# Block-causal attention with a bilinear feed-forward behind it: the softmax of a pair of heads written in eight short pieces, weight conversions written step by step, and constant products in the first five slots

## The chip, the cores and the metric

The kernel runs on one core of one Trainium2 chip. The metric is device time in microseconds (us) of one execution, the median of several runs. Lower is better.

## The reference

Sixty-four heads (8 batches of 8) attend over 576 positions of width 64, with a mask that lets a block of 64 queries see its own block and those before it. The heads of a position are put side by side, and a bilinear feed-forward of width 1536 follows.

```python
scores = scale * np.matmul(q, k.transpose(0, 1, 3, 2))
scores = np.where(block_i >= block_j, scores, -1000000000.0)   # blocks of 64
scores = scores - np.max(scores, axis=-1, keepdims=True)
attn = np.exp(scores)
attn = attn / (np.sum(attn, axis=-1, keepdims=True) + 1e-09)
attn_out = np.matmul(attn, v).astype(np.float32)
x = attn_out.transpose(0, 2, 1, 3).reshape(4608, 512)
a = x @ w_a            # 512 x 1536
b = x @ w_b            # 512 x 1536
return (a * b @ w_out).astype(np.float32)
```

## The kernel before

The heads go through in 32 pairs, two heads of 64 features on the 128 partitions. A loop over 34 **slots** (`for s in range(NP + LAG)`, L571) does three things in each slot `s`: the output products of pair `s-2` (`values`, L459), the transposes of pair `s-1` (`turn`, L437) and the scores and softmax of pair `s` (`softmax`, L366). Each of the three is a Python generator, and a table `SLOT` (L567) says in which order their next pieces are written; the third number of an entry is its weight in the slot's progress `now`, which runs from `2s` to `2s+2`.

Between the pieces stand products of the feed-forward's **first pass** (`first_pass`, L493): the first 4 of 12 blocks of 128 hidden features, for 16 half batches of 288 positions. For each block f, `ab_unit` (L234) makes a sum of 12 products for `a` and one of 12 for `b` in two PSUM banks of `ps_mm` (2 buffers, tag `mm`): ScalarE copies the first to SBUF (`a`, L247), VectorE multiplies the second with it (`hf`, L249), ScalarE rounds that (`hh`, L112), GpSimd takes the rest (`hl`, L115). After the first block of a half batch stand the output products of the half batch before (`o_unit`, L254), four sums of 12 products that ScalarE copies out (`ob`, L502). As there are two buffers, a new sum waits until the sum but one before has been read. `want(now)` (L555) sets how many products have been written at a given `now`: none before 10.2 (`MOE_FROM`, in slot 5), and 72 in each slot from slot 9 on. Slots come in two kinds by turns: one holds the second, third and fourth block of a half batch (six sums called `ps`), the other holds a first block and the output products (two `ps`, four `pso`).

In a slot, `softmax` writes first the scores of query tile 3 (`LAST`), of the side tile (`NT`, 64 queries at each end) and of tile 1, in four banks of `ps_sc` (L399 to L403). VectorE takes the row maxima (`top`, L388, tile `nm`; `nb` for tiles that share rows, L411), ScalarE the exponentials with their row sums (`exps`, L391): tile 3 of both heads (out `e`, bias `nb`, 128x512), the side tile of both (out `e_s`), then tile 1 (`e`, bias `nm`, 128x320) after a masking memset (L395). The second piece writes the scores of tiles 2 and 0 in the same four banks, their maxima and exponentials (128x448, 128x192), the reciprocals of the sums (`rc`, L430) and GpSimd's scaling of all exponentials by them (L434). `turn` is in seven pieces: up to four transposes with the identity (`tp`, L453, two buffers) and ScalarE's copy of them (`ah`, L456). `values` makes `av` (L471) from `ah` and `v`.

Pairs 0 to 5 use plain fp32 products for the scores (`NATIVE`), later pairs split q and k into rounded and rest parts (`split_qk`, L342: L348, L349 for q, L112, L115 for k).

The weights of the first pass are **converted** on the way in (`convert`, L129: five VectorE operations of 128x512 on a block and one ScalarE operation, then a rounding copy on ScalarE and a subtraction on VectorE, L110). They are 12 conversions of 5 steps; `CONV_PER_SLOT`, `CONV0` and the loop at L595 set how many steps have been written at a given `now`.

TensorE's instructions stand in program order (`PE_ORDER`, L542). The other engines' queues are ordered by a scheduler, which may put an instruction of later code ahead of one of earlier code; each engine then runs its queue in order. Before the loop stand 9 products of zeros into a `ps_mm` bank (`WARM`, L309).

After slot 33 come the rest of the first pass and the second pass (L769 on), which the change doesn't touch.

Of the kernel before, what the change touches and what calls it, by code (L numbers as in the profile page):

```python
# [9 lines left out]
F32 = mybir.dt.float32  # L10
# [7 lines left out]
P = 128  # L18
BLK = 64
NEG = -1.0e30  # L20
EPS = 1e-9
CONV_POOL = 1
CONV_POOL2 = 0
CONV_PER_SLOT = 1.0
CONV0 = 1
HL_DVE = False
MOE_FROM = 10.2
# [4 lines left out]
XQ = lambda nc: nc.scalar  # L32
PE_ORDER = ["PE"]
WARM = 9
KEEP = {}
NATIVE = 6

XFB = 2
# [16 lines left out]
def attention_then_bilinear_ffn(  # L55
# [10 lines left out]
    nc = tc.nc  # L66
# [202 lines left out]
    ps_t = psum(right, "ps_t", 1)  # L269
# [10 lines left out]
    nk = [min(P * t + 3 * BLK, S - BLK) for t in range(NT)]  # L280
# [4 lines left out]
    W = S - BLK  # L285
# [18 lines left out]
    if WARM:  # L304
        z = const.tile([P, W], F32R, name="z")
        nc.vector.memset(f32(z), 0.0)
        ps = ps_mm.tile([P, 512], F32, tag="mm", name="warm")
# [58 lines left out]
    def softmax(p):  # L366
# [3 lines left out]
        eb = [e_bufs[(2 * p + h) % NE] for h in range(2)]  # L370
        sm = s_bufs[p % 2]

        nm, rc = (apool.tile([P, 2, NT + 1], F32, tag=x, name=f"{x}{n}") for x in ("nm", "rc"))
        nb = apool.tile([P, 2, 2], F32, tag="nb", name=f"nb{n}")

        def banks(t):
            return [ps_sc.tile([P, 512], F32, tag="sc", name=f"s{t}{n}_{h}") for h in range(2)]

        def scores(t, outs):
            for j, (qq, kk) in enumerate(qk):  # L380
                for h, r in enumerate(rows):
                    keys = ends(kk[r]) if t == NT else kk[r, :nk[t]]
                    mark = nc.tensor.matmul(  # L383
                        outs[h], qq[r, q0[t]:q0[t] + P], keys, start=j == 0, stop=j == len(qk) - 1)
            return mark

        def top(t, h, view):
            nc.vector.tensor_reduce(nm[:, h, t:t + 1], view, axis=AX.X, op=ALU.max, negate=True)  # L388

        def exps(t, h, out, view, bias):  # L390
            nc.scalar.activation(out, view, AF.Exp, bias=bias, accum_out=sm[:, h, t, :1])  # L391

        def masked(t, ps):
            for h in range(2):
                nc.vector.memset(ps[h][:BLK, nk[t] - BLK:nk[t]], NEG)  # L395
                top(t, h, ps[h][:, :nk[t]])
                exps(t, h, eb[h][0][t][:, :nk[t]], ps[h][:, :nk[t]], nm[:, h, t:t + 1])

        ps = {t: banks(t) for t in (LAST, 1)}  # L399
        side = [x[:, nk[1]:nk[1] + P] for x in ps[1]]  # L400
# [2 lines left out]
        mark = scores(1, [x[:, :nk[1]] for x in ps[1]])  # L403
# [9 lines left out]
            nb[BLK:], two[BLK:, :, None, :].to_broadcast([P - BLK, 2, 2, 2]), axis=AX.X, op=ALU.min)  # L413
        for h in range(2):
            exps(LAST, h, eb[h][0][LAST], ps[LAST][h], nb[:, h, :1])
        for h in range(2):
            exps(NT, h, eb[h][1], side[h], nb[:, h, 1:])
        masked(1, ps[1])
        yield mark
        ps = {t: banks(t) for t in (2, 0)}  # L420
        for t in (2, 0):
            mark = scores(t, [x[:, :nk[t]] for x in ps[t]])
        for t in (2, 0):
            masked(t, ps[t])
# [120 lines left out]
    NP = NH // 2  # L545
# [9 lines left out]
    def want(now):  # L555

        n = (now - H - LAG) * per_slot - behind
        if now < 2 * H + LAG:
# [3 lines left out]
    keep = conv2 = None  # L562


    S_, T_, V_ = softmax, turn, values

    SLOT = [(V_, -2, 0), (S_, 0, 12), (T_, -1, 7), (T_, -1, 7), (T_, -1, 8), (S_, 0, 12), (T_, -1, 6),  # L567
            (T_, -1, 6), (T_, -1, 6), (T_, -1, 8)]
    fill = sum(m for _, _, m in SLOT)
    gens = {}  # L570
    for s in range(NP + LAG):  # L571
        if s == NP - 1:
            raw = fetch(wab[F1, :, 0], f"w{F1}_0")
        due = 0
        for k, (what, i, m) in enumerate(SLOT):
            i += s
            if 0 <= i < NP:
                mark = next(gens.get((what, i)) or gens.setdefault((what, i), what(i)))
                for _ in range(KEEP.get((s, k), 0)):
                    keep = keep or ps_t.tile([P, W], F32, tag="tp", name="keep", bufs=2)  # L580
                    nc.tensor.matmul(keep, z[:, :P], z, start=True, stop=True)
                marks.append(mark)
            if k == 0 and s < NP:
                load_v(s)
            if k == 5 and s + 1 < NP:
                split_qk(s + 1)
            if k == 5 and s + 2 < NP:
# [12 lines left out]
            while moe and n_moe < want(now):  # L600
                next(moe)
                n_moe += 1
# [137 lines left out]
    n_conv = n_conv2 - 1  # L740
# [8 lines left out]
    k = 0  # L749
# [16 lines left out]
    k = 0  # L766


    for ps_ in range(2):  # L769
        fs = list(range(F1 + ps_ * F2, F1 + (ps_ + 1) * F2))  # L770
        for tt in range(NT2):
# [23 lines left out]
            nm = f"z{ps_}_{tt}"  # L795
# [74 lines left out]
```

## Time and profile before

| | |
|---|---|
| median of 3 runs | 1299.45 us (1296.85 to 1302.84) |
| the profiled execution, its own time | 1300.42 us |
| its span, first to last instruction | 1298.6 us |
| TensorE (PE) busy | 1208.5 us, 93% |
| VectorE (DVE) busy | 790.7 us, 61% |
| ScalarE (ACT) busy | 620.6 us, 48% |
| GpSimd (POOL) busy | 351.9 us, 27% |
| DMA queues, mean | 104 GB/s |
| slots 0 to 33, until the last `av` ends | to 683.7 us |
| of it before the first pass's products are dense | to 128.6 us |

A row of a timeline has the start (us from the span's start), the duration, engine, line, operation, output<-inputs with the buffer numbers left out, and in brackets how long the engine had been idle before it and what released it. PEld is TensorE's weight load. A row of the waits has the waiting instruction, what it waited for, the total, how often, and the longest. A row of the windows view has a stretch, its length, the busy time of each engine with its number of instructions, the clock granted to TensorE as a share of full speed (PEclk), and the DMA load.

### The profile page before, as it was taken

What the parts mean: (1) busy time and instruction counts of PE and PEld (TensorE: products, weight loads), DVE (VectorE), ACT (ScalarE), POOL (GpSimd) and SP (SyncE); (2) the same over time, 40 slices, a digit from 0 to 9 for tenths busy, and PEclk for the clock granted to TensorE, in tenths of its full rate; (3) what the DMA queues carried; (4) which work ended last, traced back from release to release, by engine and by line L of the source; (5) the groups of instructions that cost most, each with busy time, mean ns of one, the idle gap of its engine ahead of it and who ended that gap; (6) DMA issues with size and microseconds to landing.
All of it is one profiled execution on the core that took longest, in us unless ns stands there. A gap on an engine that the chain in (4) does not pass through costs nothing.

```text
span 1298.6 us, 22050 instructions
## 1 busy us (share of the span) xinstructions
PE 1208.5 (93%) x8045; PEld 1098.4 (85%) x8045; DVE 790.7 (61%) x1932; ACT 620.6 (48%) x1550; POOL 351.9 (27%) x540
## 2 busy tenths in 40 slices
PE   5778998999999898999999989999999999999998
PEld 2446877778787787787889989999999999999998
DVE  6884444434344434444347999797788677677664
ACT  3656666565665656565554544453343322222210
POOL 1464454454535353444430001210220100000000
PEclk6677999999999999999999989999999999999999
DMA  5431222222222132212114426643668751353231
GB/s 188 135 127 49 77 87 68 86 59 77 68 86 80 57 95 68 86 59 77 39 54 138 138 80 173 157 119 98 159 162 275 213 147 51 96 147 89 58 97 61
DMA packets 68652, 135.65 MB, mean 104 GB/s; under 512 B 7616, under 2 KB 42432, under 8 KB 68544
## 3 DMA queue, kind: packets, MB, share of 16 engines
q1 hardware_dynamic: 57024, 115.37, 28.8%
q0 software_dynamic: 6912, 9.44, 4.7%
q10 hardware_dynamic: 4608, 9.44, 1.9%
q8 instruction: 63, 1.03, 0.4%
q14 instruction: 45, 0.37, 0.1%
HBM read 87.03 MB, written 47.19 MB: 103 GB/s over the span
## 4 chain that ended last, share of the span: by engine, by line
PE 74%; DVE 11%; ACT 11%; issue 3%; DMA 1%; SPq 0%; ACTq 0%; DVEq 0%
PE pso_z L722 14%; PE ps L223 9%; PE psw_z L676 7%; PE psx_z L676 7%; PE av L471 7%; PE pso L223 7%; PE psv_z L676 7%; PE s L383 6%; ACT e L391 6%; PE tp L453 5%; DVE nm L388 4%; PE psy_z L676 3%; ACT ah L456 2%; ACT e_s L391 1%; ACT a L247 1%
## 5 line engine op out<-in xcount | busy, mean ns | idle before, releaser
L223 PE MATMUL ps<-xh,wab 128*128 128x288 f32 x1024 | 230.4, 304 | 18.0 <-ACT a L247 18.0
L722 PE MATMUL pso_z<-h_z,wo 128*128 128x384 f32 x1152 | 204.3, 335 | 2.1 <-DVE u_z L703 2.1
L722 PEld LDWEIGHTS pso_z<-h_z,wo 128*128 128x128 f32 x1152 | 200.5, 188 | 2.5 <-issue 2.3
L223 PEld LDWEIGHTS ps<-xh,wab 128*128 128x128 f32 x1024 | 168.5, 188 | 28.4 <-ACT a L247 22.9
L434 POOL TENSOR_SCALAR e<-e,rc 128x512 f32<-128x512 f32 (+3 forms) x256 | 149.2, 602 | 129.5 <-DVE rc L430 127.8
L223 PE MATMUL ps<-xl,wab 128*128 128x288 f32 x512 | 158.5, 310 | 0.0
L456 ACT COPY ah<-tp 128x512 f32<-128x512 f32 x224 | 134.3, 604 | 40.0 <-PE tp L453 40.0
L388 DVE TENSOR_REDUCE nm<-s 128x1 f32<-128x512 f32 (+4 forms) x320 | 146.8, 484 | 10.3 <-PE s L383 6.3
L453 PE MATMUL tp<-ident,e 128*128 128x128 f32 x832 | 134.2, 285 | 9.9 <-ACT ah L456 6.9
L383 PE MATMUL s<-k,q 64*128 64x512 f32 (+3 forms) x900 | 113.1, 369 | 26.2 <-ACT e L391 25.8
L112 ACT CAST h_z<-u_z 128x384 fp32r<-128x384 f32 x96 | 49.3, 513 | 175.0 <-DVE u_z L701 159.6
L223 PE MATMUL pso<-hh,wo 128*128 128x288 f32 x480 | 106.1, 302 | 20.9 <-ACT ob L502 13.0
L383 PEld LDWEIGHTS s<-k,q 64*128 64x128 f32 x900 | 78.7, 193 | 52.4 <-ACT e L391 37.2
L453 PEld LDWEIGHTS tp<-ident,e 128*128 128x128 f32 x832 | 105.3, 146 | 18.7 <-issue 8.9
L785 POOL DMA_DIRECT2D part<-pt x48 | 42.6, 1056 | 288.6 <-ACT pt L784 288.4
L391 ACT ACTIVATE e<-s,nm 128x448 f32<-128x448 f32 (+2 forms) x192 | 102.5, 540 | 38.2 <-DVE nm L388 37.9
L676 PE MATMUL psx_z<-xh,wab 128*128 128x384 f32 x384 | 117.3, 341 | 3.5 <-DVE u_z L694 1.8
L676 PE MATMUL psw_z<-xh,wab 128*128 128x384 f32 x384 | 116.8, 339 | 0.0
L676 PE MATMUL psv_z<-xh,wab 128*128 128x384 f32 x384 | 116.1, 338 | 0.0
L480 DVE COPY xf<-av 128x512 f32<-128x512 f32 x32 | 22.1, 691 | 138.7 <-PE av L471 138.1
L471 PE MATMUL av<-ah,v 128*64 128x64 f32 (+4 forms) x768 | 99.4, 410 | 3.0 <-ACT ah L456 3.0
L223 PEld LDWEIGHTS pso<-hh,wo 128*128 128x128 f32 x480 | 78.5, 188 | 26.5 <-ACT ob L502 15.6
(112 smaller groups left out, 2284.3 us busy)
## 6 DMA issues: line engine op xcount, KB each, us to landing
xr<-xd SPq DMA_DIRECT2D x48, 384.0 KB, 4.4
raww<-wab SPq DMA_DIRECT2D x24, 512.0 KB, 3.8
v<-vm SPq DMA_DIRECT2D x64, 160.0 KB, 3.9
xd<-xf ACTq DMA_DIRECT2D x32, 288.0 KB, 3.8
part<-ob SPq DMA_DIRECT2D x64, 144.0 KB, 3.1
part<-pt POOLq DMA_DIRECT2D x48, 192.0 KB, 6.9
pt<-part SPq DMA_DIRECT2D x48, 192.0 KB, 3.4
outT<-pt SPq DMA_DIRECT2D x48, 192.0 KB, 3.5
```

What stands on the lines that cost most here:

```text
L112: nc.scalar.copy(hi, src)
L223: mm = nc.tensor.matmul(ps, w_, d_, start=(i == 0), stop=(i == n - 1))
L383: mark = nc.tensor.matmul(outs[h], qq[r, q0[t]:q0[t] + P], keys, start=j == 0, stop=j == len(qk) - 1)
L388: nc.vector.tensor_reduce(nm[:, h, t:t + 1], view, axis=AX.X, op=ALU.max, negate=True)
L391: nc.scalar.activation(out, view, AF.Exp, bias=bias, accum_out=sm[:, h, t, :1])
L434: nc.gpsimd.tensor_scalar(ev, ev, rc[:, h, t:t + 1], 1.0, op0=ALU.mult, op1=ALU.mult)
L453: mark = nc.tensor.transpose(tp[:, c], src, ident)
L456: nc.scalar.copy(ah[(slice(None), *at)], got)
L471: mark = nc.tensor.matmul(out[r], v[:, i, c], a[:, i, src, cols], start=start, stop=stop, skip_group_check=True)
L676: nc.tensor.matmul(ps, wt[:, i, iw], j[:, ix], start=start and kp == 0 and i == 0 and j is xh, stop=kp == KP - 1 and i == 1, skip_group_ch ...
L722: nc.tensor.matmul(ps, wt[:, a, osl], b, start=i == 0, stop=i == 3 * len(fs) - 1)
L785: nc.gpsimd.dma_start(part[o * P:(o + 1) * P, ts], t, accum_op=ALU.add)
```

## The change

`softmax` yields seven more times than at its scores' ends alone, so that it comes in eight pieces: tile 3 of the one head and all the scores and maxima before it; tile 3 of the other head; the side tiles and tile 1 of the first head; tile 1 of the second; the scores of tiles 2 and 0 with tile 2 of the first head; tile 2 of the second; tile 0 of the first; tile 0 of the second with the reciprocals and the scaling. The new `SLOT` has 16 entries (1 of `values`, 8 of `softmax`, 7 of `turn`), and products of the first pass stand behind each but the first; their number for a slot is the same. `split_qk` and `load_qk` come after the sixth piece instead of after the second. The steps of the weight conversions are written one by one at 4.4 for a unit of `now`, none before the loop; before, they came five at a time, with five ahead. `KEEP` adds products of zeros of 128x512 in one `ps_mm` bank behind every piece: three in slot 0, one in slots 1 to 4, 87 in all.

```diff
-CONV_PER_SLOT = 1.0
+CONV_PER_SLOT = 0.88
-KEEP = {}
+KEEP = [3, 1, 1, 1, 1]
...
-        def masked(t, ps):
-            for h in range(2):
-                nc.vector.memset(ps[h][:BLK, nk[t] - BLK:nk[t]], NEG)
-                top(t, h, ps[h][:, :nk[t]])
-                exps(t, h, eb[h][0][t][:, :nk[t]], ps[h][:, :nk[t]], nm[:, h, t:t + 1])
+        def masked(t, h, ps):
+            nc.vector.memset(ps[h][:BLK, nk[t] - BLK:nk[t]], NEG)
+            top(t, h, ps[h][:, :nk[t]])
+            exps(t, h, eb[h][0][t][:, :nk[t]], ps[h][:, :nk[t]], nm[:, h, t:t + 1])
...
         for h in range(2):
             exps(LAST, h, eb[h][0][LAST], ps[LAST][h], nb[:, h, :1])
+            yield mark
         for h in range(2):
             exps(NT, h, eb[h][1], side[h], nb[:, h, 1:])
-        masked(1, ps[1])
+        masked(1, 0, ps[1])
+        yield mark
+        masked(1, 1, ps[1])
         yield mark
...
-        for t in (2, 0):
-            masked(t, ps[t])
+        for t, h in ((2, 0), (2, 1), (0, 0), (0, 1)):
+            masked(t, h, ps[t])
+            if (t, h) != (0, 1):
+                yield mark
...
-    SLOT = [(V_, -2, 0), (S_, 0, 12), (T_, -1, 7), (T_, -1, 7), (T_, -1, 8), (S_, 0, 12), (T_, -1, 6),
+    S1, T1 = (S_, 0), (T_, -1)
+    SLOT = [(V_, -2, 0), (*S1, 6), (*S1, 5), (*T1, 5), (*S1, 5), (*T1, 5), (*S1, 5), (*T1, 6),
...
-                for _ in range(KEEP.get((s, k), 0)):
-                    keep = keep or ps_t.tile([P, W], F32, tag="tp", name="keep", bufs=2)
+                for _ in range(KEEP[s] if s < len(KEEP) else 0):
+                    keep = keep or ps_mm.tile([P, 512], F32, tag="mm", name="keep")
                     nc.tensor.matmul(keep, z[:, :P], z, start=True, stop=True)
...
-            if k == 5 and s + 1 < NP:
+            if k == 9 and s + 1 < NP:
                 split_qk(s + 1)
...
-            while n_conv < 5 * int(now * CONV_PER_SLOT + CONV0):
+            while n_conv < int(5 * now * CONV_PER_SLOT):
```

What the change makes of the engines' queues is seen at three places. In the names, `s_4_0` is a scores bank of the first head of the pair with heads 4 and 5, `e_3` the exponentials of tile 3 and `e_s` of the side tile, `tp_2_...` and `ah_2` belong to the pair before it, and `a_0_1` is the copy of the sum `ps` of block 1.

The first is ScalarE's queue at the start of slot 22 (the pair of heads 4 and 5 in the sixth batch), before:

```order
L391 ACTIVATE e_3_109,sm_138<-s_4_0_5444,nb_4_5443 128x512
L391 ACTIVATE e_3_117,sm_138<-s_4_1_5445,nb_4_5443 128x512
L391 ACTIVATE e_s,sm_138<-s_4_0_5446,nb_4_5443 128x128
L391 ACTIVATE e_s,sm_138<-s_4_1_5447,nb_4_5443 128x128
L456 COPY ah_2_5502<-tp_2_3_0_5503 128x4x128
L247 COPY a_0_1_5509<-ps_4_0_1_5489 128x288
L391 ACTIVATE e_1_107,sm_138<-s_4_0_5446,nm_4_5441 128x320
L456 COPY ah_2_5502<-tp_2_3_1_5519 128x4x128
L391 ACTIVATE e_1_115,sm_138<-s_4_1_5447,nm_4_5441 128x320
L112 CAST hh_0_1_5532<-hf_0_1_5530 128x288
L456 COPY ah_2_5502<-tp_2_2_0_5539 128x4x128
```

And the same stretch of the change:

```order
L391 ACTIVATE e_3_109,sm_138<-s_4_0_5532,nb_4_5531 128x512
L391 ACTIVATE e_3_117,sm_138<-s_4_1_5533,nb_4_5531 128x512
L460 COPY ah_2_5580<-tp_2_3_0_5581 128x4x128
L247 COPY a_0_1_5589<-ps_4_0_1_5568 128x288
L391 ACTIVATE e_s,sm_138<-s_4_0_5534,nb_4_5531 128x128
L391 ACTIVATE e_s,sm_138<-s_4_1_5535,nb_4_5531 128x128
L460 COPY ah_2_5580<-tp_2_3_1_5604 128x4x128
L112 CAST hh_0_1_5620<-hf_0_1_5618 128x288
L460 COPY ah_2_5580<-tp_2_2_0_5629 128x4x128
L391 ACTIVATE e_1_107,sm_138<-s_4_0_5534,nm_4_5529 128x320
L391 ACTIVATE e_1_115,sm_138<-s_4_1_5535,nm_4_5529 128x320
```

The copy `a` stands behind two exponentials instead of four, and both exponentials of tile 1 have moved behind `hh` and three copies `ah`.

The second is the same queue a little later, from tile 2 on, before:

```order
L391 ACTIVATE e_2_108,sm_138<-s_4_0_5553,nm_4_5441 128x448
L391 ACTIVATE e_2_116,sm_138<-s_4_1_5554,nm_4_5441 128x448
L348 ACTIVATE q_0_5601<-qr_0_5602 128x640
L391 ACTIVATE e_0_106,sm_138<-s_4_0_5555,nm_4_5441 128x192
L391 ACTIVATE e_0_114,sm_138<-s_4_1_5556,nm_4_5441 128x192
L247 COPY a_0_2_5606<-ps_4_0_2_5536 128x288
```

And of the change:

```order
L391 ACTIVATE e_2_108,sm_138<-s_4_0_5641,nm_4_5529 128x448
L391 ACTIVATE e_2_116,sm_138<-s_4_1_5642,nm_4_5529 128x448
L348 ACTIVATE q_0_5679<-qr_0_5680 128x640
L247 COPY a_0_2_5662<-ps_4_0_2_5624 128x288
L391 ACTIVATE e_0_106,sm_138<-s_4_0_5643,nm_4_5529 128x192
L391 ACTIVATE e_0_114,sm_138<-s_4_1_5644,nm_4_5529 128x192
```

The copy `a` of the next block has moved ahead of the two exponentials of tile 0. In the slots with output products, `ob` stands where this `a` does.

The third is TensorE's queue in slot 1, from the last scores of the first half to the first of the second, before:

```order
L383 MATMUL s_2_1_291<-k_2_162,q_2_164 128x320
L453 MATMUL tp_0_3_0_319<-ident,e_3_109 128x128 x4
L453 MATMUL tp_0_3_1_325<-ident,e_3_117 128x128 x4
L453 MATMUL tp_0_2_0_331<-ident,e_2_108 128x128 x4
L383 MATMUL s_2_0_337<-k_2_162,q_2_164 128x448
```

And of the change:

```order
L383 MATMUL s_2_1_299<-k_2_162,q_2_164 128x320
L586 MATMUL keep<-z 128x512 x2
L457 MATMUL tp_0_3_0_325<-ident,e_3_109 128x128 x4
L586 MATMUL keep<-z 128x512 x2
L457 MATMUL tp_0_3_1_345<-ident,e_3_117 128x128 x4
L586 MATMUL keep<-z 128x512 x2
L457 MATMUL tp_0_2_0_357<-ident,e_2_108 128x128 x4
L586 MATMUL keep<-z 128x512
L383 MATMUL s_2_0_365<-k_2_162,q_2_164 128x448
```

Seven products of zeros now stand between the two groups of scores, in the order of the queue. In slot 0 there are twelve at this place and twelve behind the second group. From slot 5 on TensorE's queue holds the same instructions in nearly the same order as before; the transposes stand between two products earlier and five later.

More of the change, by code (lines that the diff above doesn't have):

```diff
@@ L565, in attention_then_bilinear_ffn @@
     S_, T_, V_ = softmax, turn, values
-    SLOT = [(V_, -2, 0), (S_, 0, 12), (T_, -1, 7), (T_, -1, 7), (T_, -1, 8), (S_, 0, 12), (T_, -1, 6),
-            (T_, -1, 6), (T_, -1, 6), (T_, -1, 8)]
+    S1, T1 = (S_, 0), (T_, -1)
+    SLOT = [(V_, -2, 0), (*S1, 6), (*S1, 5), (*T1, 5), (*S1, 5), (*T1, 5), (*S1, 5), (*T1, 6),
+            (*S1, 6), (*S1, 5), (*T1, 5), (*S1, 5), (*T1, 5), (*S1, 5), (*T1, 5), (*T1, 4)]
     fill = sum(m for _, _, m in SLOT)
@@ L584, in attention_then_bilinear_ffn @@
                 load_v(s)
-            if k == 5 and s + 1 < NP:
+            if k == 9 and s + 1 < NP:
                 split_qk(s + 1)
-            if k == 5 and s + 2 < NP:
+            if k == 9 and s + 2 < NP:
                 load_qk(s + 2)
```

## Prediction

> **What bounds the kernel now.** I read the chain of waits first, for where the slots begin: each has one `av`. From slot 9's to slot 31's, 22 slots of 20.9 us, they are alike:
>
> ```profile
> 186.01 2.85 PE av L471 x24
> ...
> 645.67 2.85 PE av L471 x24
> ```
>
> The windows view of one slot of each kind:
>
> ```profile
> 374.50:395.45 20.95, 19.21 (x156) 16.57 (x158) 8.86 (x30) 12.84 (x37) 8.86 (x15) 1.00 0.25 75
> 395.45:416.43 20.98, 19.14 (x157) 16.51 (x158) 8.96 (x30) 12.88 (x37) 10.39 (x17) 1.00 0.25 75
> ```
>
> The columns are PE, PEld, DVE, ACT and POOL busy, then TensorE's granted clock. TensorE works 19.2 of 20.95 us at full clock, the others 13 at most: TensorE bounds these slots, and what it does not work is 1.8 us. The waits of PE from 186 to 646 us name all of that:
>
> ```profile
> PE ps L223 <- ACT a L247: 18.0, 21, 1.2
> PE pso L223 <- ACT ob L502: 13.0, 11, 1.2
> PE pso L223 <- ACT a L247: 7.3, 11, 0.9
> ```
>
> Together they are 38.3 us in 43 waits: two in each of 22 slots, 1.74 us a slot. Each is a new sum that waits for ScalarE to empty a bank. Before 128 us it is different; here is the windows view of slots 1 to 4, and five microseconds at the end of slot 1:
>
> ```profile
> 24.50:44.50 20.00, 15.89 (x48) 9.84 (x48) 15.65 (x47) 12.94 (x39) 8.41 (x12) 0.50 0.33 103
> 44.50:66.50 22.00, 15.58 (x72) 8.76 (x72) 18.34 (x46) 13.19 (x35) 10.45 (x14) 0.69 0.43 140
> 66.50:88.50 22.00, 14.46 (x72) 8.64 (x72) 19.00 (x46) 13.73 (x37) 11.34 (x15) 0.77 0.41 130
> 88.50:107.80 19.30, 15.85 (x72) 8.84 (x72) 10.93 (x32) 12.38 (x34) 10.51 (x16) 0.68 0.24 77
> 45.00:50.00 5.00, 5.00 (x30) 2.09 (x28) 4.62 (x7) 1.56 (x4) 5.00 (x7) 0.71 0.41 134
> ```
>
> TensorE has half its clock for much of the time, though it is busy 79% of slot 1; it gets the full clock within the one stretch that is filled (5.00 of 5.00 us). VectorE, with the conversions, works 18 to 19 of 22 us in slots 2 and 3. Behind slot 33 the change touches nothing, so I add nothing there.
>
> **The dense slots.** TensorE's order hardly moves, so the question is when ScalarE ends what TensorE waits for. I walk through the slot at 374.50 with ScalarE's rows:
>
> ```profile
> 382.22 0.36 ACT L391 ACTIVATE e_s<-s,nb 128x128 f32<-128x128 f32 x1
> ...
> 382.90 0.59 ACT L456 COPY ah<-tp 128x512 f32<-128x512 f32 x1
> 383.37 0.43 ACT L247 COPY a<-ps 128x288 f32<-128x288 f32 x1
> 383.66 0.57 ACT L391 ACTIVATE e<-s,nm 128x320 f32<-128x320 f32 x1
> 384.08 0.24 ACT L391 ACTIVATION_READ_ACCUMULATOR e<-s,nm 128x1 f32 x1
> 384.17 0.62 ACT L456 COPY ah<-tp 128x512 f32<-128x512 f32 x1
> ...
> 387.59 0.63 ACT L391 ACTIVATE e<-s,nm 128x448 f32<-128x448 f32 x1 [1.46 <-DVE nm L388]
> ...
> 388.82 0.73 ACT L348 ACTIVATE q<-qr 128x640 fp32r<-128x640 f32 x1
> 389.45 0.41 ACT L391 ACTIVATE e<-s,nm 128x192 f32<-128x192 f32 x1
> ...
> 390.24 0.40 ACT L247 COPY a<-ps 128x288 f32<-128x288 f32 x1
> ...
> 394.44 0.59 ACT L456 COPY ah<-tp 128x512 f32<-128x512 f32 x1 [0.35 <-PE tp L453]
> ```
>
> and TensorE's of the same slot:
>
> ```profile
> 383.85 0.40 PE L223 MATMUL ps<-xh,wab 128*128 128x288 f32 x1 [0.56 <-ACT a L247]
> ...
> 385.82 1.20 PE L383 MATMUL s<-k,q 64*128 64x448 f32 x12
> ...
> 390.69 0.40 PE L223 MATMUL ps<-xh,wab 128*128 128x288 f32 x1 [1.18 <-ACT a L247]
> ...
> 395.03 0.29 PE L223 MATMUL ps<-xl,wab 128*128 128x288 f32 x1
> 395.16 0.29 PE L223 MATMUL ps<-xh,wab 128*128 128x288 f32 x1
> 395.38 1.08 PE L471 MATMUL av<-ah,v 128*64 128x512 f32 x4
> ```
>
> *First wait.* TensorE was ready at 383.29 (383.85 less 0.56). The two `e_s`, with their reading of sums, take 382.22 to 382.90, 0.68 us, and stand behind `a` in the change. So `a` starts at 382.69, ends 0.43 later at 383.12, and TensorE goes on 0.05 later as before (383.80, 383.85): at 383.17, before it is ready. The 0.56 are gone, with 0.1 to spare. In the other kind of slot it is `pso` that waits, for the same copy.
>
> *What comes late instead: the second scores.* Their second half goes into the banks that the two `e` of tile 1 read. In the change these two stand behind `e_s` twice (0.68 from 382.98), the next `ah` (0.47, 382.90 to 383.37), `hh` (about 0.32) and another `ah` (0.47): they start at about 384.95 and, a step of 0.51 later (383.66 to 384.17), 385.46. The second is done with its sum 0.66 later (383.66 to 384.32), at 386.12. VectorE's `hf` now stands ahead of their maxima, but that ends by 384.6. TensorE begins these scores 0.56 sooner, at 385.26, and is half way (of 1.20) at about 386.0. New wait: 0.15.
>
> *Second wait.* The `e` of tile 2 moves 0.56 forward with its scores, to 387.03. To `q` it is 1.23 as before (388.26), `q` takes 0.63, then `a` at once: 388.89, done 0.40 later, TensorE goes on at 389.34. It would be ready at 390.69 - 1.18 - 0.56 + 0.15 = 389.10. Of 1.18 there are 0.24 left.
>
> *The slot's end.* From that sum to `av` it is 4.69 us, so 394.03. The last transposes stand four products nearer to `av` (0.13 each, 395.03 to 395.16; four are 0.53). The `ah` made of them ended 0.35 before `av` (394.44 + 0.59, against 395.38); now it is 0.18 late. GpSimd's scaling starts 0.3 sooner and is needed in the next slot only; the scores of q and k split by the moved `split_qk` are two slots away. Both cost nothing, and their cover is a whole slot.
>
> So 1.74 becomes 0.15 + 0.24 + 0.18 = 0.57, a gain of 1.17 a slot, **25.7 us in 22 slots**. Bounds: all 38.3 go, or only the first wait goes (0.56 by 22, 12.3). Slots 6 to 8 and 31 have fewer products and other small waits; I give them 0, with 2 either way.
>
> **The first six slots.** The conversions: though written later, VectorE's queue has six, three and three of them ahead of the first three `xf` copies (L480) in both kernels, so they cost and save nothing. The constant products are like the nine before the loop (the first row, from the groups), and part of them falls into waits of PE: the second row is slot 0's in the timeline, the third those of slots 1 to 4 (24.5 to 107.8 us).
>
> ```profile
> L309 PE MATMUL warm<-z 128*128 128x512 f32 x9 | 4.2, 646 | 1.5 <-DVE z L306 1.5
> ```
>
> ```profile
> 19.67 2.53 PE L383 MATMUL s<-k,q 64*128 64x448 f32 x4 [11.56 <-ACT e L391]
> ```
>
> ```profile
> PE s L383 <- ACT e L391: 12.9, 8, 4.3
> ```
>
> One takes 4.2 / 9 = 0.47 us on a cold clock, so about 0.23 on a full one. In slot 0 the first twelve lie in the wait for exponentials of 11.56 us; the second twelve (5.6 us cold) push the next scores, while VectorE has conversions to do: I count +3. In slots 1 to 4 there are 63: 29.6 us cold, 14.5 warm; about half stand ahead of the second scores, in the 12.9. At full clock the half-clock share of these slots (100%, 62%, 46%, 64% of 20, 22, 22, 19.3 us, about 80% of it busy) saves up to 22 us of TensorE, but VectorE holds slots 2 and 3 to 18 or 19 of 22 us. I take -4, -2, -2 and -4 with the products counted, and +3 for slot 0: -9; as I have no row that shows that the clock stays up, two thirds of it, **-6**. Bounds: -16 (clock up from slot 1), and +20: cold, 29.6 less the 12.9 of waits, and 5.6 less what VectorE covers, some 2.
>
> The Trainium skill, "TensorE: Matmul & The Clock Gate", section "Part 1: The HAM clock gate", says the clock rises after a busy window of about 3.4 us and falls after an idle one. The trace agrees that a filled stretch raises it (the row at 45 us), and its slot 1 adds that 79% does not. By the page's rule the longest wait of 4.3 us, with seven products in it, is no longer an idle window, and the sum would take -16 in place of -6: 1257 us.
>
> **The sum** is made against the profiled execution's own time, 1300.4 us: less 25.7 and 6 it is 1268.7. That execution lay 1 us above the median of 1299.45, so I forecast **1268 us**.
>
> **The rivals.** *A, the clock stays up and all waits go:* 1299.5 - 38 - 16 = 1245; with the clock alone, and 25.7 in the dense slots, 1257. For it speak the seven products in the 4.3 us wait; against it slot 1 and VectorE's 19 of 22 us. Chance 0.17. *B, only the first wait goes,* because `a` and `ob` still stand behind `q` and both exponentials of tile 2, whose start hangs on the scores: 1299.5 - 12.3 - 6 = 1281. Chance 0.17. *C, the constant products run cold and lie on the path:* 1299.5 - 25.7 + 20 = 1294. Chance 0.08. *D, slower: the second scores take over the wait.* Both exponentials of tile 1 wait for maxima behind `hf`, which waits for a sum and for `a`; each microsecond that the second of them is late beyond 386.0 stops TensorE in each of 22 slots. From 1.6 us (instead of 0.15) it eats the 25.7 and the 6; at 2 us it is 1299.5 - 6 - 25.7 + 22 x 1.85 = 1308. My walk speaks against it by 1.4 us. Chance 0.05. That the change does nothing is no rival: the queues differ.
>
> **How the numbers follow.** The forecast has 0.53, with a range of its own from 1260 to 1277. The range of 1250 to 1292 takes in B and the clock part of A, and leaves out C, D and the end of A. About 0.5% (6.5 us) can be told from no change. Forecast, A and B are faster: 0.87; C lies at the bound, so 0.07 for the same and 0.06 for slower.
>
> **What would show it.** In the profile after: `av` each 19.8 us in the dense slots, PE busy 97% there; the waits for `a` and `ob` fallen from 38 to some 5 us, with small new rows, `s` for `e` (3 us) and `av` for `ah` (4 us); PEclk above 0.8 in slots 2 to 4, and the first dense slot some 6 us earlier. I am wrong in the walk if the wait of `s` for `e` is above 1 us a slot or `a` keeps its 1.2, and wrong on the clock if slots 1 to 4 stay at half.

## The result, and the profile after

| | median, us | range | ratio to before, 95% |
|---|---|---|---|
| before, same session | 1300.45 | 1296.85 to 1302.84 | |
| the change | 1278.44 | 1277.34 to 1279.51 | 0.983 [0.981, 0.986] |

The change gains 22 us; 32 were forecast, and 1278 lies in the range. The page of the profile after (span, busy time, and the clock in fortieths of the span):

```profile
span 1275.5 us, 22228 instructions
...
PE 1229.0 (96%) x8132; PEld 1114.6 (87%) x8132; DVE 789.1 (62%) x1932; ACT 622.8 (49%) x1550; POOL 353.5 (28%) x540
...
PEclk7888999999999999999999999999999999999999
```

The span fell from 1298.6 by 23.1 us. Where? The chain of waits gives the `av` of slots 9 and 31:

```profile
186.04 2.09 PE av L475 x9
...
621.60 2.52 PE av L475 x13
```

Slot 9 begins where it did (186.01 before). The 22 dense slots take 435.56 us instead of 459.66: **all of the gain, 24.1 us, is there**. From slot 31 to the end it is 1.0 longer. The view of the waits of PE between those two rows has these two and no other:

```profile
PE av L475 <- ACT ah L460: 1.4, 9, 0.2
PE pso L223 <- ACT a L247: 0.8, 2, 0.6
```

The three rows with 38.3 us have shrunk to 0.8. Two slots in the windows view show what is left idle, 0.28 us of each:

```profile
364.70:384.34 19.64, 19.36 (x154) 16.63 (x154) 8.81 (x31) 12.85 (x37) 8.75 (x14) 1.00 0.24 74
384.34:404.20 19.86, 19.58 (x154) 16.65 (x154) 8.85 (x30) 12.90 (x38) 10.56 (x19) 1.00 0.27 86
```

The early slots, 1 to 5, and all the dense ones in the windows view of after:

```profile
24.60:46.50 21.90, 18.92 (x76) 13.31 (x75) 16.68 (x48) 13.20 (x39) 9.13 (x13) 0.78 0.33 106
46.50:68.00 21.50, 17.46 (x88) 10.90 (x88) 18.25 (x45) 13.51 (x36) 10.97 (x13) 0.84 0.38 131
68.00:91.06 23.06, 18.18 (x88) 11.68 (x89) 19.16 (x47) 13.81 (x36) 11.07 (x14) 0.78 0.37 124
91.06:111.04 19.98, 17.80 (x88) 11.72 (x88) 10.79 (x31) 11.87 (x33) 8.92 (x14) 0.83 0.23 75
111.04:129.73 18.69, 17.58 (x127) 13.64 (x127) 8.98 (x30) 12.87 (x36) 9.81 (x17) 1.00 0.22 68
...
186.04:621.60 435.56, 428.77 (x3388) 365.76 (x3388) 194.17 (x660) 282.17 (x812) 213.06 (x334) 1.00 0.25 77
```

Slot 5 and the dense slots of before, in the same view:

```profile
107.85:128.55 20.70, 19.98 (x129) 14.44 (x131) 8.84 (x30) 12.15 (x35) 9.47 (x17) 0.88 0.22 61
...
186.01:645.67 459.66, 421.32 (x3390) 363.51 (x3392) 195.57 (x659) 281.75 (x812) 211.80 (x333) 1.00 0.25 73
```

In the dense slots TensorE's busy time rose by 7.5 us, from 421.32 to 428.77. It stands in one group: the second scores of each slot, twelve products. Here they are with the sum that follows, after, and then the sum that followed them before (there they started at 385.82):

```profile
375.39 1.66 PE L383 MATMUL s<-k,q 64*128 64x448 f32 x12
376.97 0.40 PE L223 MATMUL ps<-xl,wab 128*128 128x288 f32 x1
```

```profile
386.95 0.40 PE L223 MATMUL ps<-xl,wab 128*128 128x288 f32 x1
```

From their start to the next sum's it is 1.58 us where it was 1.13, and so in each of the 22 slots (means 1.59 and 1.12). The group starts on time and then stops within: its weight loads wait for the exponentials of tile 1, in a row that the kernel before does not have:

```profile
PEld s L383 <- ACT e L391: 7.2, 22, 0.3
```

So the change has a new wait for `e` of 0.47 us a slot, 10.3 in all, and most of it counts as busy.

In slots 1 to 4 the clock did rise: 0.78, 0.84, 0.78 and 0.83, where it was 0.50, 0.69, 0.77 and 0.68. Yet TensorE is busier (18.18 us in slot 3, where it was 14.46), and the slots are not shorter. Slot by slot against before, from the starts of `av`: slots 0 and 1 together +2.0 us (46.51 against 44.52), slot 2 -0.8, slot 3 +1.2, slot 4 +0.8, slot 5 -2.0, slots 6 to 8 -1.2: zero in all. The question for the experiments is therefore double: is the gain of the dense slots the walk's, and why does a better clock give nothing here?

### The profile page after: what moved, and what is told of

It is laid out like the page before. It is cut to its first block, busy times and chain, and to the rows that moved or that the text cites. A ratio compares the mean times of both kernels' runs of the same rounds, so it can differ in the third digit from the quotient of the medians.

```text
span 1275.5 us, 22228 instructions
## 1 busy us (share of the span) xinstructions
PE 1229.0 (96%) x8132; PEld 1114.6 (87%) x8132; DVE 789.1 (62%) x1932; ACT 622.8 (49%) x1550; POOL 353.5 (28%) x540
## 4 chain that ended last, share of the span: by engine, by line
PE 74%; ACT 12%; DVE 10%; issue 3%; DMA 1%; POOL 0%; SPq 0%; ACTq 0%; DVEq 0%
PE pso_z L727 15%; PE ps L223 9%; PE psw_z L681 8%; PE psx_z L681 8%; PE psv_z L681 7%; PE av L475 7%; PE pso L223 6%; PE tp L457 5%; PE s L383 5%; ACT e L391 5%; ACT ah L460 4%; PE psy_z L681 4%; DVE nm L388 3%; ACT e_s L391 2%; PE keep L586 1%
## 5 line engine op out<-in xcount | busy, mean ns | idle before, releaser
L383 PE MATMUL s<-k,q 64*128 64x512 f32 (+3 forms) x900 | 118.1, 367 | 27.4 <-ACT e L391 24.7
L457 PE MATMUL tp<-ident,e 128*128 128x128 f32 x832 | 130.8, 278 | 0.1
L223 PE MATMUL pso<-hh,wo 128*128 128x288 f32 x480 | 112.5, 311 | 0.8 <-ACT a L247 0.8
L475 PE MATMUL av<-ah,v 128*64 128x64 f32 (+4 forms) x768 | 93.6, 393 | 6.6 <-ACT ah L460 4.5
L223 PEld LDWEIGHTS ps<-xl,wab 128*128 128x128 f32 x512 | 96.4, 188 | 1.6 <-issue 0.4
```

Of the source, the lines that this page charges most:

```text
L223: mm = nc.tensor.matmul(ps, w_, d_, start=(i == 0), stop=(i == n - 1))
L383: mark = nc.tensor.matmul(outs[h], qq[r, q0[t]:q0[t] + P], keys, start=j == 0, stop=j == len(qk) - 1)
L457: mark = nc.tensor.transpose(tp[:, c], src, ident)
L475: mark = nc.tensor.matmul(out[r], v[:, i, c], a[:, i, src, cols], start=start, stop=stop, skip_group_check=True)
```

## The experiments

All twelve in one table. "Slot 9" is the start of its `av` (186.01 before, 186.04 after), "dense" the 22 slots from there (459.66 and 435.56), each read from the one profiled execution of the kernel. From slot 31 to the end the change, `e1`, `e2` and `e7` to `e12` hold the same instructions, yet their traces take from 651.7 to 655.7 us there; so a few us of a median belong to no edit, and the early slots are judged by slot 9. Medians of before beside them were 1299.0, 1297.7, 1299.3 and 1298.7 us in the order of the groups (`e1` to `e4`, `e5` to `e8`, `e9` to `e11`, `e12`).

| run | what it is | median, us | ratio, 95% | slot 9 | dense |
|---|---|---|---|---|---|
| e1_no_products | change without products | 1275.28 | 0.981 [0.980, 0.983] | 184.08 | 435.2 |
| e2_products_ahead | products only ahead of the second scores | 1270.40 | 0.978 [0.976, 0.980] | 180.60 | 434.8 |
| e3_pieces_alone | pieces alone | 1276.83 | 0.983 [0.981, 0.985] | 185.05 | 435.4 |
| e4_no_pieces | all but the pieces | 1293.59 | 0.996 [0.994, 0.997] | 181.70 | 460.0 |
| e5_first_half | only the first four pieces cut | 1290.51 | 0.995 [0.993, 0.996] | 183.75 | 450.3 |
| e6_second_half | only the last four pieces cut | 1293.11 | 0.996 [0.995, 0.998] | 187.65 | 450.7 |
| e7_wait_filled | waits filled with products | 1274.05 | 0.983 [0.981, 0.985] | 183.70 | 435.2 |
| e8_late_conversion | the same, conversions late on VectorE | 1270.11 | 0.979 [0.978, 0.981] | 177.99 | 434.9 |
| e9_late_faster | e8 with a faster pace | 1269.71 | 0.977 [0.976, 0.979] | 177.71 | 435.3 |
| e10_late_few | e9 with the products of e2 | 1261.00 | 0.972 [0.970, 0.974] | 171.88 | 434.9 |
| e11_late_no_products | e8 without products | 1265.49 | 0.975 [0.973, 0.976] | 175.87 | 434.8 |
| e12_change_late | the change, conversions late | 1269.10 | 0.977 [0.974, 0.981] | 177.87 | 435.0 |

### The parts one by one

The first takes the products away:

```diff
-KEEP = [3, 1, 1, 1, 1]
+KEEP = []
```

> The changed kernel without the 87 constant products (KEEP empty); the eight pieces and the step-by-step conversions stay. Theory 1 (the dense slots 9 to 30 give all of the gain, and in slots 0 to 4 what the constant products gain by the clock is about what they cost on TensorE's path): 1278 us, within 4, the av of slot 9 near 186 us, and PEclk of slots 1 to 4 back near 0.66. Rival 2 (the products are what cost the forecast early gain): 1270 us or less. Rival 3 (they do gain by the clock, and something else costs it): 1284 us or more.

It took 1275.28 us: the products cost 2 us net by slot 9, 3 by the medians. With what stood in front of the second scores gone, the timeline shows TensorE's wait there in slot 2:

```profile
56.21 2.53 PE L383 MATMUL s<-k,q 64*128 64x448 f32 x4 [5.46 <-ACT e L391]
```

In the changed kernel slot 2 reads:

```profile
57.84 2.53 PE L383 MATMUL s<-k,q 64*128 64x448 f32 x4 [3.00 <-ACT e L391]
60.95 1.51 PE L383 MATMUL s<-k,q 64*128 64x192 f32 x4 [0.59 <-ACT e L391]
62.40 1.22 PE L586 MATMUL keep<-z 128*128 128x512 f32 x2
63.41 1.05 PE L457 MATMUL tp<-ident,e 128*128 128x128 f32 x4
64.12 1.19 PE L586 MATMUL keep<-z 128*128 128x512 f32 x2
```

The seven products fill about half of the wait; 3.00 us stay, the clock falls at 58.3 us, just behind them (TensorE worked 0.51 of the 3.42 us before that), and the scores take 2.53 us as without any products. Then come pairs of products at 1.2 us on a half clock, in a stretch in which TensorE waits for nothing: these lie on the path. So the second run keeps only the products ahead:

```diff
-for _ in range(KEEP[s] if s < len(KEEP) else 0):
+for _ in range(KEEP[s] if s < len(KEEP) and k < 8 else 0):
```

> The changed kernel with the constant products ahead of the second scores alone (12 in slot 0, seven or eight in each of slots 1 to 4); those behind them, 2 to 4 us on a half clock in each slot, are left out. Theory 1 with its reason (the products behind the second scores lie on the path, and the clock falls in the wait ahead of these scores whatever stands behind them): 1278 less 4 to 10, so 1268 to 1274 us. Rival 3 (the products behind are what lifts the clock for av and the next scores): 1278 us or more, with av and the first scores on a half clock.

1270.40 us, 8 less than the change. Slot 9 starts at 180.60: the 43 products ahead gain 3.5 us against none (184.08), and the 44 behind cost 5.4 (186.04). (Of the rest of the 8 us, 2.2 lie behind slot 31, where both kernels are the same.) The clock of slots 2 to 4 owes the latter nothing:

```profile
41.61:63.15 21.54, 17.22 (x80) 10.10 (x80) 17.42 (x44) 12.95 (x35) 9.42 (x14) 0.76 0.39 129
63.15:84.07 20.92, 15.63 (x81) 9.61 (x81) 18.02 (x46) 13.38 (x36) 10.18 (x14) 0.84 0.41 136
84.07:104.69 20.62, 15.77 (x80) 9.54 (x81) 15.14 (x39) 13.41 (x36) 10.18 (x14) 0.83 0.32 101
```

Its mean is 0.81 where the change has 0.82, with 1.6 us a slot less work (48.62 against 53.44 busy in the three).

The pieces alone, with the old pace of the conversions as well:

```diff
-CONV_PER_SLOT = 0.88
+CONV_PER_SLOT = 1.0
-KEEP = [3, 1, 1, 1, 1]
+KEEP = []
-            while n_conv < int(5 * now * CONV_PER_SLOT):
+            while n_conv < 5 * int(now * CONV_PER_SLOT + CONV0):
```

> The kernel before with the eight pieces alone: no constant products, conversions as before (five steps at a time, five ahead). Theory 1 (the scheduler takes the conversions ahead of the softmax whenever they are written, so their pace does nothing): the same as e1_no_products within 2 us. Rival 4 (the slower pace of the conversions takes work off VectorE in slots 1 to 3): 3 to 8 us slower than e1_no_products.

1276.83 us, and its interval overlaps that of the first run: the pace of writing conversions does 1.5 us or nothing. That no step is written before the loop does not show on the engine: without the edits to the pace, and with them, VectorE begins with a conversion (at 10.04 and 9.88 us; more below). And the counterpart, the change without its pieces (the kernel before with these edits):

```diff
-CONV_PER_SLOT = 1.0
+CONV_PER_SLOT = 0.88
-KEEP = {}
+KEEP = [3, 1, 1, 1, 1]
-                for _ in range(KEEP.get((s, k), 0)):
-                    keep = keep or ps_t.tile([P, W], F32, tag="tp", name="keep", bufs=2)
+                for _ in range(KEEP[s] if s < len(KEEP) else 0):
+                    keep = keep or ps_mm.tile([P, 512], F32, tag="mm", name="keep")
-            while n_conv < 5 * int(now * CONV_PER_SLOT + CONV0):
+            while n_conv < int(5 * now * CONV_PER_SLOT):
```

> The kernel before with the constant products (three behind every piece in slot 0, one in slots 1 to 4, 44 in all as there are fewer pieces) and the step-by-step conversions, but softmax in two pieces and the old table of slots. Theory 1: 1300 us within 4, dense slots of 20.95 us. Rival (a part of the 22 us comes from the first slots): 1290 us or less.

1293.59 us, between the two expectations. Dense slots as before (460.0), slot 9 at 181.70: behind ten coarser pieces there are only 45 products, of which slot 0 has 6, and with the pace they gain 4.3 us. In the split kernel the same setting makes 87, and its gain is gone.

### Both halves of the cut are needed

Two runs cut only one of the two parts of `softmax`; the other keeps its coarse place, by weights of zero in `SLOT`:

```diff
-            (*S1, 6), (*S1, 5), (*T1, 5), (*S1, 5), (*T1, 5), (*S1, 5), (*T1, 5), (*T1, 4)]
+            (*S1, 0), (*S1, 0), (*S1, 0), (*S1, 11), (*T1, 10), (*T1, 10), (*T1, 5), (*T1, 4)]
```

> The changed kernel with only the first four pieces apart: the last four are written together where the fifth stands, so ScalarE's queue has a ahead of e_s, but the next a (or ob) behind both exponentials of tile 0 as before. By the walk of the prediction the first wait goes (0.56 a slot) and everything to the second copy moves forward by as much: 22 slots x 0.5 to 0.56, 11 to 12 us, so 1287 to 1290 us against 1278 for the change and 1300 for the kernel before; the row of PE waiting for ob and for the second a keeps about 1 us a slot. Rival (the two waits are one loop, and either edit frees the whole of it): below 1282 us.

1290.51 us, 0.5 above what was expected: dense 450.3, a gain of 9.3 or 0.42 a slot. The waits of PE in its dense slots are

```profile
PE pso L223 <- ACT ob L506: 8.0, 11, 0.7
PE ps L223 <- ACT a L247: 7.2, 10, 0.7
PE av L475 <- ACT ah L460: 1.1, 7, 0.2
PE pso L223 <- ACT a L247: 0.5, 1, 0.5
```

One wait a slot, as walked: the first is gone, the second stays with 0.7. TensorE's idle time falls by 16.5 us, to 21.8, and its busy time rises by 7.2, to 428.5: the late second scores are there in full (1.59 us from their start to the next sum's), so they are the price of this half.

The other way round:

```diff
-    SLOT = [(V_, -2, 0), (*S1, 6), (*S1, 5), (*T1, 5), (*S1, 5), (*T1, 5), (*S1, 5), (*T1, 6),
+    SLOT = [(V_, -2, 0), (*S1, 0), (*S1, 0), (*S1, 0), (*S1, 11), (*T1, 10), (*T1, 10), (*T1, 6),
```

> The changed kernel with only the last four pieces apart: the first four are written together where the first stands, so a is behind e_s as before, and the next a (or ob) stands ahead of the exponentials of tile 0. By the walk: the first wait of 0.56 stays, the second copy comes 0.79 sooner (two exponentials of 0.39), the slot ends 0.6 to 0.8 sooner: 13 to 17 us, 1282 to 1287 us. Rival as for e5: below 1282 us; if it gives 1290 or more, the first half carries the gain.

1293.11 us, short of what the walk said (1282 to 1287): dense 450.7, 0.41 a slot.

```profile
PE ps L223 <- ACT a L247: 10.2, 21, 0.6
PE pso L223 <- ACT a L247: 7.9, 11, 1.4
PE pso L223 <- ACT ob L506: 4.3, 11, 0.4
PE av L475 <- ACT ah L460: 1.5, 10, 0.2
```

In the slots with output products the second wait (`ob`) is down from 13.0 to 4.3 us, as walked, and the first is still there (7.9, 7.3 before); in the other slots two waits are left in the first row, of 0.5 each. The halves give 9.3 and 8.9, together 18.2; both at once give 24.1. They do not simply add. Of the 5.9 us between, 2.4 are idle time (less by 16.5 and 12.6 alone, by 31.5 together) and 3.5 busy time (more by 7.2 and 3.7 alone, by 7.5 together). The second scores are not late in this run (1.13 us), and why its busy time rises by 3.7 stays open. I read the idle part so that the second half of a slot starts from where ScalarE's queue stands after the first, but no run tries that alone.

### Why the better clock gives so little

If half clock and waits bound the early slots, filling each wait wholly should shorten them:

```diff
-KEEP = [3, 1, 1, 1, 1]
+KEEP = [12, 2, 3, 3, 2]
-for _ in range(KEEP[s] if s < len(KEEP) else 0):
+for _ in range(KEEP[s] if s < len(KEEP) and k < 8 else 0):
```

> The changed kernel with constant products ahead of the second scores alone, and more of them: twelve behind each of the four pieces there in slot 0, two behind each in slots 1 and 4, three in slots 2 and 3, none behind the second scores. Theory (the clock falls in the wait ahead of the second scores; filled, it stays up to slot 5): PEclk 0.9 or more in all of the first 130 us, slots 1 and 4 shorter by 3 to 4 us each than in e2_products_ahead, and 1262 to 1268 us. Rival (VectorE, not TensorE, ends these slots last): the clock is up but the time is that of e2_products_ahead, 1270 us, within 2. Second rival (the products delay the second scores): above 1272 us.

1274.05 us: the theory misses. The second rival has the number, but not the reason: in slot 0 the second scores start at 19.94 us, where they start at 19.92 with the few products. The clock came, 0.92 in slots 2 to 4, but slots 2 and 3 are only 0.8 and 0.2 us shorter than with the few products ahead (21.54 and 20.92, at 0.76 and 0.84), and slots 0 and 1 are 6.0 longer:

```profile
47.64:68.41 20.77, 17.90 (x96) 11.52 (x97) 19.88 (x47) 13.42 (x36) 12.22 (x14) 0.92 0.45 156
68.41:89.12 20.71, 18.36 (x97) 11.90 (x97) 14.84 (x38) 12.74 (x34) 10.79 (x14) 0.92 0.36 116
```

So TensorE's speed is not what sets these two. The chain of waits through them, 41.5 us long, lies for about 20.6 us on VectorE, 13.4 of these in conversions, for 13.5 on ScalarE, and for 5.1 on TensorE. The other slots differ in conversions too, for the scheduler placed them otherwise: VectorE makes seven of the twelve (counted by L151) in slots 0 and 1, where the kernel with the few products has four, and is busy 35.6 us there instead of 27.6; in slot 4 it makes none instead of two, and that slot is shorter, 17.8 us against 20.6. The timeline at 28 us, in slots 0 and 1, shows how a conversion holds up TensorE; rows of three engines:

```profile
28.18 0.67 DVE L149 SCALAR_TENSOR_TENSOR sw<-raww,sw 128x512 int32<-128x512 int32 x1
28.77 0.60 DVE L388 TENSOR_REDUCE nm<-s 128x1 f32<-128x448 f32 x1
...
29.41 0.63 ACT L391 ACTIVATE e<-s,nm 128x448 f32<-128x448 f32 x1 [1.98 <-DVE nm L388]
...
30.23 2.81 PE L383 MATMUL s<-k,q 64*128 64x512 f32 x4 [5.59 <-issue]
```

VectorE works through a conversion (its last step here is L149) before it takes the row maximum of scores that are there; ScalarE's exponential waits 1.98 us for that maximum; the next scores need the bank that the exponential reads, and TensorE stands still for 5.59 us. (The view names no releaser here; the order of the three ends is the reason for this reading.) A loop of scores, maximum, exponential, next scores sets these slots, as I read it, and the conversions stand in it, on VectorE. The next run leaves the code's order and alters where the scheduler may put a conversion: each step must stand behind the last maximum (`nb`) written before it on VectorE.

```diff
-KEEP = [12, 2, 3, 3, 2]
+KEEP = [7, 2, 3, 3, 2]
-            if paced:
-                behind_of(ins, "hf")
+            behind_of(ins, "hf" if paced else "nb")
```

> As e7_wait_filled, with seven instead of twelve products a piece in slot 0, and each step of the weight conversions placed on VectorE behind the nb of the pair before it in the program (a dependency that sets the order alone), so that they do come step by step and VectorE does not wait 8.2 us for the first weights with scores lying ready. Theory (the early slots end with VectorE): slot 0 is 4 to 6 us shorter and the time 1256 to 1264 us. Rival (TensorE and latency bound them): the time of e7_wait_filled within 2 us.

1270.11 us, 6 short of the expectation, but slot 2 starts at 34.48 instead of 47.64. (Not by the order alone: slot 0 has 20 products of zeros less, and VectorE makes three conversions in slots 0 and 1 instead of seven. The order alone is tried in the last two runs.) Some of it is given back in slots 5 and 6, into which conversions now fall (22.4 and 21.4 us, where the change has 18.7 and 19.0). The next three runs ask for the shares. A faster pace:

```diff
-CONV_PER_SLOT = 0.88
+CONV_PER_SLOT = 1.2
```

> The kernel with filled waits and conversions that stand behind their pair's last maximum, with the pace of the conversions raised from 0.88 to 1.2, so that the steps that fell into slots 5 and 6 stand in slots 0 to 4. Theory: slots 5 and 6 lost 22.4 - 18.7 and 21.4 - 19.0, about 6 us, to conversions on VectorE; earlier slots are bound by TensorE at half clock or by the scores' wait and take more conversions for less; 1264 to 1267 us. Rival: VectorE's work sets the length of every early slot, so it only moves; 1269 to 1272.

1269.71 us: the rival. Slot 6 is 19.0 us again and slots 2 and 5 are shorter too, but slots 0 and 1 are 3.0 us longer (slot 2 starts at 37.45 instead of 34.48) and slot 3 takes 21.5 us instead of 19.3. VectorE's work only moved.

That with the products of the second run:

```diff
-KEEP = [7, 2, 3, 3, 2]
+KEEP = [3, 1, 1, 1, 1]
```

> The same with three products ahead of the second scores' steps in the first slot and one in each of the next four, in the place of 7, 2, 3, 3, 2. Theory that the clock sets the first slots: the waits are left open, the clock falls again, and the first nine slots are longer by 3 to 5 us than with the filled waits. Rival, that VectorE's queue sets them: within 1.5 us of the filled one.

1261.00 us, the fastest kernel of this study: 8.7 us less than with the waits filled, 5.8 of them until slot 9 and 3.9 behind slot 31; neither theory said so. The waits of PE from 37 to 116 us with the filled waits (e9):

```profile
PE tp L456 <- ACT ah L459: 6.8, 7, 2.1
PE av L474 <- ACT ah L459: 5.3, 4, 2.8
PE s L382 <- ACT e L390: 1.9, 4, 1.2
```

and with the few products (e10):

```profile
PE s L382 <- ACT e L390: 6.7, 5, 2.4
PE av L474 <- ACT ah L459: 2.7, 4, 1.0
PE tp L456 <- ACT ah L459: 1.8, 1, 1.8
```

The filled kernel waits no less (14.0 us against 11.2), only elsewhere: the scores no longer wait, the transposes and `av` do. TensorE's timeline of slot 3 in the filled kernel:

```profile
60.84 1.89 PE L382 MATMUL s<-k,q 64*128 64x512 f32 x12
62.66 1.66 PE L585 MATMUL keep<-z 128*128 128x512 f32 x6
...
69.52 2.01 PE L382 MATMUL s<-k,q 64*128 64x448 f32 x8
...
74.63 0.52 PE L456 MATMUL tp<-ident,e 128*128 128x128 f32 x3 [2.07 <-ACT ah L459]
```

and in the one with few products:

```profile
60.42 1.89 PE L382 MATMUL s<-k,q 64*128 64x512 f32 x12
62.24 0.73 PE L585 MATMUL keep<-z 128*128 128x512 f32 x2
...
65.37 1.65 PE L382 MATMUL s<-k,q 64*128 64x448 f32 x4
```

From the first scores to the second it is 8.7 us with 21 products between them (60.84 to 69.52) and 4.9 us with seven (60.42 to 65.37). That these products make the slot longer is not shown. The chain of waits of the filled kernel's slot 3 (57.08 to 78.55) has 0.9 us of products, those ahead of the first scores; from 62.0 us to the end it runs through VectorE and ScalarE alone, and a conversion's step (L148, 72.02) still stands ahead of a maximum in it. VectorE also works more in that slot, 17.75 us against 13.23. So why fewer products do better here stays open between the products and the conversions that moved with them.

The late order at the pace of the change, without any products:

```diff
-KEEP = [7, 2, 3, 3, 2]
+KEEP = []
```

> Conversions behind their pair's last maximum at the pace 0.88, and no products at all. Theory that both count: the gain of the queue order alone, from slots 0 and 1 that were 10 us shorter and slots 5 and 6 that were 5 us longer, about 5 us against the nine pieces without products (1275), so 1270 to 1273, and the first nine slots 3 to 5 us longer than with the products. Rival, that products alone made the gain: 1275 or more.

1265.49 us: better than either expectation. Without any products the late order gives 8.2 us at slot 9 (184.08 to 175.87) and some 10 in the medians. Slots 0 and 1 give 6.6 us of that and slots 2 to 4 give 7.4; slots 5 and 6, into which conversions now fall, take back 5.7. VectorE's timeline shows where the first part comes from, first without the late order (e1):

```profile
9.88 0.43 DVE L141 TENSOR_SCALAR sw<-raww 128x512 int32<-128x512 int32 x1 [8.47 <-DMA raww<-wab]
...
13.07 0.68 DVE L388 TENSOR_REDUCE nm<-s 128x1 f32<-128x512 f32 x1
```

and with it (e11):

```profile
7.69 1.29 DVE L387 TENSOR_REDUCE nm<-s 128x1 f32<-128x512 f32 x2 [6.29 <-PE s L382]
```

In the one, VectorE's first instruction of the slots is a conversion whose weights come at 9.9 us, and the first maximum is taken at 13.07; in the other the first maximum is taken at 7.69, as soon as its scores are there. The last run changes only this in the changed kernel:

```diff
-            if paced:
-                behind_of(ins, "hf")
+            behind_of(ins, "hf" if paced else "nb")
```

> The changed kernel with one thing altered: each step of a conversion stands behind its pair's last maximum on VectorE. Theory: the order of VectorE's queue and the products act on their own, so the late order gives what it gave without products (about 10 us) and the products behind the second scores' steps keep their price: 1266 to 1270 us, first nine slots about 10 us shorter. Rival: with the conversions out of the way the scores' waits are short, the products behind cost more than they did, and the sum is 1271 or more.

1269.10 us, within the expectation (its four runs spread from 1265.45 to 1274.28), slot 9 at 177.87, 8.2 earlier than in the change. With both orders of VectorE's queue, then, slot 9 starts at 184.08 / 180.60 / 186.04 (no products, ahead only, everywhere) and at 175.87 / 171.88 / 177.87: the order is worth 8.2 to 8.7, the products ahead gain 3.5 to 4.0, those behind cost 5.4 to 6.0. (The middle one of the second three has the faster pace too, which moved slot 9 by 0.3 between e8 and e9.) As far as single traces show it, the two causes add.

## Why the prediction was right in the dense slots and wrong in the early ones

- **What bounds the dense slots:** right. Waits of 38.3 us of PE for `a` and `ob` are gone, and nothing else was needed: with the pieces alone the dense slots are 24.3 us shorter.
- **First wait and second wait:** right in direction, and each wait fell to nothing instead of 0 and 0.24 (0.8 us in all 22 slots). Tried alone, the first half of the cut takes away the first wait and the second half most of the second. But the walk took the two as separate, and alone they give 0.42 and 0.41 a slot, where I had 0.56 and 0.94 less the new waits.
- **Second scores late (0.15):** right in kind, mis-sized: it is 0.47 a slot, in every slot. No row of PE shows it, since the wait lies inside the group of scores; the row of PEld does. **`av` late (0.18):** up to 0.2, but in 9 slots of 22, 0.06 on the mean.
- **The slots:** 1.10 us shorter each, 1.17 forecast. The idle time fell by more than forecast, from 38.3 to 6.8 us (435.56 less 428.77 busy) where 12.5 were expected, but TensorE's busy time rose by 0.34 a slot with the same instructions, which is the wait inside the second scores. That the two numbers lie so near is luck in part: the second wait and `av` cost less than the walk had, the second scores three times as much. It is these slots that keep the total in the range.
- **Conversions 0:** right as a price of the edit, since the two paces give 1275.28 and 1276.83. But the same queue held a gain of 8 us that I passed over, since I asked only whether the edit moves the conversions, and not what they cost where they stand.
- **The first six slots, -6:** this is the step that failed. It gave 0.0: slots 6 to 8, put at 0, gained 1.2, and slots 0 to 5 lost 1.2. The sum that I made of it was a clock that rises, less TensorE's share of the cold products. The clock rose about as hoped: between 7 and 113 us it was at half for 75 us before, and for 44 us after, by the clock's own records. But (1) a faster TensorE hardly shortens a slot that is set by scores, maximum, exponential and the next scores (the filled waits, clock 0.92, slots 2 and 3 of 20.8 and 20.7 us); I had written "VectorE holds slots 2 and 3" and priced it as a limit of busy time (19 of 22), while it acts through order. And (2) I put the products that lie on the path into a net figure of -4, -2, -2, -4 without a row for them; the 44 behind the second scores cost 5.4 us by themselves, against 3.5 gained by the 43 ahead.
- **Rival A,** by which the clock would stay up: its clock part fell. By the rule that I drew on there (the Trainium skill, "TensorE: Matmul & The Clock Gate", section "Part 1: The HAM clock gate": full clock after a busy window of about 3.4 us, half after an idle one) I had counted the 4.3 us wait as broken up by seven products. The trace agrees with the length of the window, since every change of the clock lies a multiple of 3.4 us from the next. It does not agree that only an idle window lowers it: in the changed kernel the clock fell at 58.3 and 78.8 us after 3.4 us with 15% and 26% of work, but at 37.9 and 102.7 us after 3.4 us with 50% and 51%. So both the rule and my count failed: in slots 2 and 3 the products left 3.0 and 3.4 us of wait (of 5.5 and 5.7 without products, `e1`), and in slots 1 and 4 waits of 1.3 us at most were enough. With the waits filled its mean was 0.92 in slots 2 to 4, and the time did not follow.
- **Rivals B, C and D** fell for the dense slots (B, D) and in size (C: the products do lie partly on the path, at 5.4 us and not 20).

## What to carry to other kernels

An exponential or a copy that a full engine waits for is worth moving by half a microsecond when it recurs in every slot; cut a long step into pieces so that the queue can take the awaited copy between them, and walk both halves of a slot together. Where a slot is a loop through several engines, a clock or a busy share of one of them is no price: look which instruction stands ahead of the awaited one in each queue. A wait can hide inside a group that counts as busy: where busy time grows with the same instructions, look at the waits of the weight loads. Filling products belong into a wait and nowhere else; the same setting that gains ahead of the second scores costs behind them.

## What the runs showed of the hardware

- The clock granted to TensorE was only ever 0.5 or 1.0 in the records, and its stretches were multiples of 3.4 us (in the changed kernel full for 10.2, half for 6.8, full for 13.7, half for 6.8, full for 13.7 us, from 27.6 us on). Products of zeros raise it like others: with the waits filled (`e7`), PEclk in the first three slices of the page is 8, 9 and 8, where it is 7, 6 and 7 without products (`e1`).
- The clock also fell after stretches in which TensorE worked most of the time: with the waits filled (`e7`) at 83.7 us, after 3.41 us with 2.24 us of work, in which TensorE's longest wait was 0.76 us.
- Two products of zeros of 128x512 took 0.73 us on full clock and 1.22 on half, a factor of 1.7. In longer rows it is near the clock's 2: eleven took 2.65 us on full clock (`e7`, at 15.81 us), 0.24 each, and the nine before the loop 4.2 us on half (before), 0.47 each.
